# Another issue sequence for an attention and softplus-FFN kernel on one core

## The chip, the cores and the metric

The kernel runs on one core of a Trainium2 chip. The metric is the device time of one execution in microseconds (us), from several executions. A core has engines that each work through their own instruction stream in order: TensorE (PE, matmuls; its weight loads are listed as PEld), VectorE (DVE), ScalarE (ACT), GpSimd (POOL) and SyncE (SP), on whose queue this kernel issues all of its DMAs.

## The reference

Attention over 4 batches, 8 heads, 768 positions of 64, then a feed-forward network (FFN) on the 3072 tokens of 512 values, in fp32:

```python
k_sum = k.reshape(B, H, nb, block, D).max(axis=3)      # block = 32, nb = 24
v_sum = v.reshape(B, H, nb, block, D).mean(axis=3)
scores_l = scale * np.matmul(q, k.transpose(0, 1, 3, 2))
mask_l = np.abs(pos[:, None] - pos[None, :]) < window   # window = 16
scores_s = scale * np.einsum('bhsd,bhnd->bhsn', q, k_sum) + np.log(block)
scores_all = np.concatenate([np.where(mask_l, scores_l, -1e9), scores_s], axis=-1)
a = np.exp(scores_all - scores_all.max(axis=-1, keepdims=True))
a = a / (a.sum(axis=-1, keepdims=True) + 1e-9)
attn = np.matmul(a, np.concatenate([v, v_sum], axis=2))
x = attn.transpose(0, 2, 1, 3).reshape(B * S, H * D)
h = x @ w_in                                            # 512 x 2048
g = np.maximum(h, 0.0) + np.log1p(np.exp(-np.abs(h)))   # softplus
out = g @ w_out                                         # 2048 x 512
```

So each query sees its 31 neighbours and 24 summaries of blocks of 32 keys (maximum) and values (mean).

## The kernel before

**Numbers and precision.** An fp32 matrix product is made from three matmuls on values split into a high part (fp32r, a shortened fp32) and a low part (the rest): high by high, low by high, high by low. The weights arrive from the host as 64-bit words and are taken apart on the chip.

**Tasks.** The program does not issue instructions as it goes. An object `Order` collects 1603 tasks, each with a number, the buffers that it reads and writes and one or two ways to run it (each way on one engine). `Order.issue(SEQUENCE)` then issues them in the order of the words of a string. A word is the number of a task; the suffix `a` picks the second way, on another engine. Waits between engines follow from the buffers. Since each engine works through its tasks in the order of issue, the string alone fixes what stands behind what on each engine and on SP's queue.

**Work and names.** The 12 chunks (256 queries each) form the groups x = 0 (two chunks), 1 (one), 2 to 5 (two each) and 6 (one). `a2.0.0` is the attention of group 2, its chunk 0, head pairs 0 and 1; `f0.8` is FFN block f = 8 of 16 for group 0; `w8` are the weights of that block; `s1` are the summaries of batch 1. The FFN runs over (group, blocks): (0, 0 to 10), (1, 0 to 10), (0, 11 to 15), (1, 11 to 15), then groups 2 to 6 with all 16 blocks each.

- Attention of a chunk and two head pairs: load q, k and v windows (SP) and the summaries (`load_sums`); `k_sums` copies the key summaries beside the keys (L490, DVE or ACT); `scores` (L582, PE); `mask` (L595, DVE); `exp` (L603, ACT); `inverse` (L610, L611, DVE); `normalize` (L616, GpSimd, or DVE as the second way); then for the first group transposes on PE (L629, L633), otherwise `transpose` on DVE (L642), a DMA out to a buffer "squares" and four back; `values` (L673, PE); `high` (L689, ACT) and `low` (L693, DVE) write the split FFN input xh, xl.
- Weights of a block: two loads of 512 KB (w_in L722, w_out L719); `magnitude` (DVE L735, or ACT L738), `clamp` (L742), `shift` (L746) and `sign` (L750) on DVE; `tail` (ACT L756 or DVE); `add_tail` (GpSimd, L764); `high` (L768, ACT or DVE) and `low` (L775, DVE or GpSimd). For w0 and w1 the w_in half and the w_out half are converted apart.
- FFN of a block: `product` (L804, PE, 12 matmuls into a PSUM bank "ph", of which there are two, shared with `values`, the warm matmuls and the first sums of v); `rounded` (L824, ACT softplus, the high part), `exact` (L828, ACT) and `rest` (L832, DVE, the low part); `project` (L841, PE) first with the high part, then with the low part. At the end of a group's blocks `read` (L872, L876) takes the result from PSUM and L893 stores it.
- Summaries of a batch: four loads of keys (L339) with a maximum on DVE (L325), four loads of values (L347, "st") with `sum_v` (L353 to L358, GpSimd, or DVE as the second way), `mean` (L365). For batch 0 the sums of v are matmuls (L403) and the mean is on ACT (L416).
- 40 tasks of two matmuls on the identity (`warm`, L915) fill TensorE at the start.

The buffers of tag "t" (two in turn) hold in turn keys or values for the summaries, the weights in conversion and results on their way out, so a load into one of them waits until the user before is done.

Of the kernel before, what the change touches and what calls it, by code (L numbers as in the profile page):

```python
# [159 lines left out]
610a 430 420 251a 423 361 587a 431 259 295 252 590 421 253 613 362 254 360 614 256 363 432 365 411 434 424 412  # L160
615 433 257a 367 258 364 594 435 591a 373 368 616 598 617 299 366 369 374 370 371 375 595a 436 376 592 627 599a
372 437 606 628 377 629 380 438 381 378 439 382 593 383 271 631 379 440 441 445 285 442 272 451 273 446 275 274
443 447 596 452 600 444 630 448 276 453 612 449 454 618 260 457 300 619 277a 463 608 458 597 278a 459 450 464
460 455 636a 465 466 456 384 261 461 385 462 265 262 386 469 263 264 639 470 471 472 475 266 654 640 620 611 481
476 477 607 305 478 609 467 291 655 658a 653 468 482 267a 473 483 641 292 474 293 479 484 480 294 487 268 493
296 488 661 485 489 676 494 490 623 495 486 642 622 297 643a 491 621 675 281a 499 496 298a 677 644 492 508 680a
282 500 283 284 501 497 509 502 286 510 498 662 301a 516 511 287a 663 288 683 512 302 804 645 503 303 805 513
# [16 lines left out]
949 957 954 1089 1090a 1091 958 955 963 960 959 1092 964 1100 965 1101 1109a 961 1071 968 1072 1079 1081 1073
1093 1094 1095 1096 974 969 1080 1082 970 1084 971 1085 980 975 1103 1102 976 1104 977 1097 966 1105 1098 1107
1099 1106 1108 1112 981 1110 982 1111 967 1113 1232 972 1236 983 1114 973 978 979 984 1115 1116a 1117 985 986
1233 1118 1237 1234 1238 992 987 1119 1120 988 1121 989 990 993 1122 994 995 998 1235a 1239a 1242 1004 999 1000
1246 1001 1249 1250 1258 1251 1010 1005 1253 1006 1252 1243 991 996 1007 1247 1240 1016 1011 1012 1244 1248 1241
1261 997 1262 1002 1013 1263 1245 1003 1008 1009 1017 1014 1264 1265a 1266 1018 1015 1123 1019 1267 1275 1276
1284 1020 1124 1277 1021 1024 1125 1279 1278 1022 1025 1254 1023 1027 1026 1126 1028a 1268 1269 1270 1271 1029  # L190
1255 1134 1127 1257 1128 1256 1259 1129 1260 1287 1135 1136 1130 1288 1131 1132 1137 1289 1133 1138 1272 1139
1280 1281 1273 1290 1140 1283 1291a 1282 1285 1274 1286 1292 1146 1141 1293 1302 1306 1303 1142 1301 1143 1144
1147 1148 1149 1152 1294 1295 1296 1297 1158 1153 1154 1155 1298 1159 1160 1309 1304 1299 1305 1300 1145 1307
1310 1150 1308 1161 1311 1151 1156 1157 1162 1312 1313a 1163 1314 1164 1315 1324 1328 1325 1323 1170 1165 1316
1166 1317 1167 1168 1318 1171 1319 1172 1173 1176 1320 1177 1178 1331 1326 1321 1179 1327 1322 1169 1329 1332
# [797 lines left out]
```

## Time and profile before

| | |
|---|---|
| three runs | 640.96, 639.19, 639.84 us; median 639.84 |
| span of the profiled execution | 638.3 us, 11177 instructions |
| PE busy | 623.1 us (98%) |
| DVE, ACT, POOL busy | 277.6 (43%), 316.3 (50%), 75.6 us (12%) |
| mean granted TensorE clock | 0.991 |
| DMA | 86.51 MB, mean 136 GB/s |

The span runs from the first to the last instruction; the runs shown are 0.9 to 2.7 us above it, the median 1.5. In the profile's rows, "start us, us, engine line op out<-in" of a timeline is followed in brackets by the idle time before it and the engine (with its tile and line) that ended it. A row of the chain of work gives start, duration and what ran. A row of the groups ends with busy us, mean ns of one, and idle time before it. 40 digits of a slice row are tenths of busy time in 40 equal slices of the span.

### The profile page before, as it was taken

To read this page: it belongs to the slowest core of one execution; us is meant where nothing else is said; L and a number is where in the kernel's file an instruction comes from. 1 tells how busy PE (TensorE), PEld (TensorE's weight loads), DVE (VectorE), ACT (ScalarE), POOL (GpSimd) and SP (SyncE) were. 2 spreads that over 40 slices of the span, in tenths; PEclk is the share of its full clock that TensorE was granted. 3 is DMA by queue.
4 is the path that set the end of the run, shared out by engine and by line. 5 is a ranking of instruction groups with operands and counts; after the bars stand their busy time and mean duration, and the time that the engine had idled before them with its cause. 6 is when DMAs were issued, how large, how long until landed. Compare 5 with 4: busy or idle time off the path is not lost.

```text
span 638.3 us, 11177 instructions
## 1 busy us (share of the span) xinstructions
PE 623.1 (98%) x4284; PEld 505.5 (79%) x4284; DVE 277.6 (43%) x753; ACT 316.3 (50%) x762; POOL 75.6 (12%) x70
## 2 busy tenths in 40 slices
PE   7889999999999999999999999999999999999997
PEld 6576777888888888887777877787888888888996
DVE  5879988779643435213451445432411111341111
ACT  4879887479652555215472434462522222552222
POOL 3333322334201130001000030000000000000000
PEclk9889999999999999999999999999999999999999
DMA  9999699744668742141354653453300400311100
GB/s 291 247 262 324 234 224 248 218 139 117 210 201 243 222 139 88 63 134 42 137 167 116 179 143 106 130 145 107 98 1 0 139 1 0 109 57 60 48 1 34
DMA packets 86629, 86.51 MB, mean 136 GB/s; under 512 B 26704, under 2 KB 72368, under 8 KB 86576
## 3 DMA queue, kind: packets, MB, share of 16 engines
q1 hardware_dynamic: 86576, 85.80, 46.2%
q8 instruction: 34, 0.56, 0.3%
q14 instruction: 19, 0.16, 0.1%
HBM read 65.01 MB, written 18.35 MB: 131 GB/s over the span
## 4 chain that ended last, share of the span: by engine, by line
PE 91%; DMA 3%; ACT 3%; SPq 1%; DVE 1%; issue 0%; ACTq 0%
PE po L841 42%; PE ph L804 41%; PE xo L673 4%; PE sc L582 3%; DMA raw<-w_out_dram 2%; DMA k<-kT_dram 1%; ACT sp L603 1%; PE vt L403 1%; DVE sp L616 1%; ACT t L738 0%; SPq L722 0%; ACT pT L633 0%; PE pt L629 0%; ACT raw L756 0%; ACT w L768 0%
## 5 line engine op out<-in xcount | busy, mean ns | idle before, releaser
L804 PE MATMUL ph<-xh,w 128*128 128x512 f32 (+1 forms) x896 | 261.7, 365 | 4.0 <-DVE gl L832 2.5
L841 PE MATMUL po<-w,gh 128*128 128x512 f32 x768 | 204.8, 396 | 0.0
L804 PEld LDWEIGHTS ph<-xh,w 128*128 128x128 f32 x896 | 161.8, 189 | 35.0 <-DVE gl L832 3.1
L832 DVE TENSOR_TENSOR gl<-ph,gh 128x512 fp32r<-128x512 f32 (+1 forms) x112 | 68.2, 611 | 232.5 <-ACT ph L828 211.2
L841 PEld LDWEIGHTS po<-w,gh 128*128 128x128 f32 x768 | 142.3, 188 | 32.7 <-issue 0.8
L804 PE MATMUL ph<-xl,w 128*128 128x512 f32 (+1 forms) x448 | 163.0, 364 | 0.5 <-DVE xl L693 0.5
L824 ACT ACTIVATE gh<-ph 128x512 fp32r<-128x512 f32 (+1 forms) x112 | 60.2, 538 | 207.3 <-PE ph L804 169.3
L841 PE MATMUL po<-w,gl 128*128 128x512 f32 x384 | 115.6, 398 | 0.0
L804 PEld LDWEIGHTS ph<-xl,w 128*128 128x128 f32 x448 | 84.6, 189 | 16.2 <-DVE xl L693 1.3
L841 PEld LDWEIGHTS po<-w,gl 128*128 128x128 f32 x384 | 71.0, 188 | 17.1 <-issue 0.9
L603 ACT ACTIVATE sp<-sp,nm 128x120 f32<-128x120 f32 x192 | 73.1, 382 | 4.4 <-DVE nm L595 4.1
L828 ACT ACTIVATE ph<-ph 128x512 f32<-128x512 f32 (+1 forms) x112 | 59.4, 531 | 0.0
L764 POOL TENSOR_TENSOR t<-t,raw 128x1024 int32<-128x1024 int32 (+1 forms) x18 | 41.8, 2328 | 91.7 <-DVE t L750 26.3
L595 DVE CUSTOM_DVE_ANT_0 sp<-sc,added 128x120 f32<-128x120 f32 x192 | 40.7, 277 | 17.7 <-PE sc L582 17.3
L824 ACT ACT_TABLE_LOAD x24 | 30.8, 1283 | 34.0 <-PE ph L804 30.7
L693 DVE TENSOR_TENSOR xl<-xo,xh 128x512 fp32r<-128x512 f32 x24 | 16.5, 689 | 46.2 <-ACT xh L689 46.2
L603 ACT ACTIVATION_READ_ACCUMULATOR sp<-sp,nm 128x1 f32 x192 | 35.9, 187 | 0.0
L689 ACT CAST xh<-xo 128x512 fp32r<-128x512 f32 x24 | 14.1, 586 | 40.9 <-PE xo L673 40.9
L616 DVE TENSOR_TENSOR sp<-sp,ss 128x960 f32<-128x960 f32 x21 | 26.4, 1258 | 0.5
L673 PEld LDWEIGHTS xo<-pT,v 120*64 120x64 f32 x640 | 20.3, 138 | 7.5 <-issue 6.2
L642 DVE STREAM_TRANSPOSE tb<-sp 128x1024 f32<-128x1024 f32 x20 | 24.8, 1240 | 1.5 <-POOL sp L616 1.2
L353 POOL TENSOR_TENSOR st<-st 96x512 f32<-96x512 f32 (+1 forms) x10 | 10.1, 1011 | 127.9 <-DMA st<-v_hp_dram 127.5
(60 smaller groups left out, 379.4 us busy)
## 6 DMA issues: line engine op xcount, KB each, us to landing
squares<-tb SPq DMA_DIRECT2D x20, 512.0 KB
pT<-squares SPq DMA_DIRECT2D x80, 128.0 KB
raw<-w_in_dram SPq DMA_DIRECT2D x16, 512.0 KB
raw<-w_out_dram SPq DMA_DIRECT2D x16, 512.0 KB
kf<-kT_dram SPq DMA_DIRECT2D x16, 384.0 KB
out_dram<-ob SPq DMA_DIRECT2D x11, 512.0 KB
q<-qT_dram SPq DMA_DIRECT2D x20, 256.0 KB
st<-v_hp_dram SPq DMA_DIRECT2D x12, 384.0 KB
```

Of the source, the lines that this page charges most:

```text
L582: nc.tensor.matmul(unit(g * NU + h * NPAIR + i)[r * QW:(r + 1) * QW, k0:k1], lhsT=q[rows, w * QW:(w + 1) * QW], rhs=k[rows], start=True, s ...
L595: nc.vector.tensor_tensor_reduce(out=sp()[:, n], in0=unit(n), in1=added()[:, kinds.index((lows[w], lows[w + 1]))], scale=-SCALE, scalar=FL ...
L603: nc.scalar.activation(sp()[:, n], sp()[:, n], AF.Exp, bias=nm()[:, n:n + 1], scale=-1.0, accum_out=ss()[:, n:n + 1],)
L616: engine.tensor_tensor(sp(), sp(), s, op=ALU.mult)
L642: nc.vector.transpose(out=tb().rearrange("p k (u q) -> p u k q", q=SQ), in_=tiles.sp().rearrange("p u (k q) -> p u k q", q=SQ),)
L673: nc.tensor.matmul(xo()[h * D:(h + 1) * D, g * CH + w * QW:g * CH + (w + 1) * QW], lhsT=tiles.v(g)[:, w, h * D:(h + 1) * D], rhs=queries(g ...
L764: nc.gpsimd.tensor_tensor(a, a, word(0, I32), op=ALU.add)
L804: nc.tensor.matmul(ph()[:, :n_x], lhsT=w1()[:, i1, part, cc * P:(cc + 1) * P], rhs=a()[:, cc, :n_x], start=cc == 0 and i == 0, stop=cc == ...
L824: nc.scalar.activation(gh()[:, :n_x], ph()[:, :n_x], AF.Softplus)
L828: nc.scalar.activation(ph()[:, :n_x], ph()[:, :n_x], AF.Softplus)
L832: nc.vector.tensor_sub(out=gl()[:, :n_x], in0=ph()[:, :n_x], in1=gh()[:, :n_x].bitcast(F32),)
L841: nc.tensor.matmul(po[t](), lhsT=a()[:, t * P:(t + 1) * P], rhs=w2()[:, i2, part], start=f == f0 and i == 0, stop=f == f1 - 1 and i == 2,)
```

## The change

Only the string SEQUENCE differs: the same 1603 tasks and the same buffers are issued in another order, and 58 of them on another engine. Read engine by engine:

- **SP.** The first w_in halves of w0 (133) and w1 (151) are issued before the first q (64, 68), two loads of v (65, 97) come earlier among the loads of the first attention, and w4 (189, 190) precedes the other loads of v. Further on, more weight loads stand ahead of the k and v loads and squares of group 1.
- **PE.** 32 of the 40 warm tasks come ahead of the first scores (72). The set of tasks before the first FFN product (309) is the same. After it some neighbours change places: 314 before 325, 329 before 331, 330 before 337, 354 before values 410, scores 613 and project 360 before product 361, project 366 before product 373. In the later groups the scores of a chunk come several products earlier than before and pieces of attention stand side by side more often: 29 separate interruptions of the FFN's matmuls instead of 36.
- **DVE and ACT.** Rest 328 (f0.2) is issued ahead of mask 400 and normalize 403 (a1.0.0); before, it came behind them. Exp 106 (a0.0.2) now follows the tail of w0's w_out half (147). ACT and DVE exchange work: magnitudes 134, 143, 191, 231, 301, highs 167, 177, 297, k_sums 396, 422, 1083, 1109, 1486 and reads 382, 1024, 1025, 1226, 1445, 1448, 1449, 1599 go from ACT to DVE; highs 140, 149, 207, 287, read 800 and k_sums 907, 1035, 1258, 1284, 1328, 1460 from DVE to ACT. Transpose 404 is moved ahead of the conversion of w6.
- **GpSimd.** From DVE it takes normalizes 76, 665, 888, 914, 1064, 1090, 1116, 1265, 1291, 1335, lows 159, 168, 288, and the sums of v 587, 591, 595, 599 (batch 1) and 1235. DVE takes from it lows 141, 278, 298, 308, sums 866, 870, 1243 and normalize 1042. GpSimd has 44 tasks instead of 34, ACT 344 instead of 354, DVE 350 as before.

The head of the diff, up to the first FFN blocks:

```diff
 SEQUENCE = """
-0 2 64 3 43 4 45 5 68 6 133 7 160 8 51 1 9 47 132 10 44 11 49 12 13 46 14 55 15 72 96 53 16 134a 138a 17 73 151
-161a 74 162 100 84 135 163 142 164 136 137 57 18 165 85 139 19 59 20 166 52 48 86 61 75 76a 65 388 50 70 77 167
-21 396a 168 104 66 78 140a 156 141a 147 79 105 69 54 189 143a 56 152a 144 87 58 106 190 153 88a 60 62 145 154
-146 22 116 63 155 80 71 107 157 23 117 24 67 25 26 97 27 148 158 28 169 29 118 30 170 31 108a 32 101 33 34 98 35
-149a 99 36 159 37 38 103 39 150 40 102 119 191a 120a 81 179 195 192 89 91 193 90 180 41 92 194 82 93 128 171a 83
-196 130 42 94 109 131 111 95 110 199 112 172 309 391 175 173 129 174 197 200 113 389 176 392 121 114 387 123 122
-115 390 124 397 198 177 125 178 318 126 181a 219 127 220 185 182 239 310 183 240 201a 184 319 311 202 186 399
-312 320 414 313 269 205 325 209 203 187 204 413 321 188 225 416 314 415 326 206 322 315 417 327 400 316 210 221a
-317 270 323 207a 208 229 401 324 222 331 223 230 224 289 245 402 403a 329 241a 328 226 422a 332 404 337 405 242
-227 279 243 249 333 228 330 338 339 425 244 395 211a 335 334 246 340 215 343 212 235 406 213 247 214 336 344 248
-341 426 216 584 345 393 342 250 601 347 346 427 602 217a 604 407 218 348 585 588 349 394 398 231a 408 428 409
-290 232 355 350 603 233 234 351 589 236 353 356 352 357 586 605 358 410 429a 237 354 418 255 238 280 359 419
-610a 430 420 251a 423 361 587a 431 259 295 252 590 421 253 613 362 254 360 614 256 363 432 365 411 434 424 412
-615 433 257a 367 258 364 594 435 591a 373 368 616 598 617 299 366 369 374 370 371 375 595a 436 376 592 627 599a
...
+133 0 3 4 5 6 7 8 9 10 11 12 134 135 43 136 45 44 46 13 14 15 16 151 138a 2 17 1 137 152a 153 154 18 64 155 68 19 20
+139 21 22 140 156 23 24 25 26 27 28 29 141 30 31 32 33 34 157 72 35 36 37 160 51 165 47 38 39 100 53 49 73 161a 40 162
+163 164 52 84 65 74 96 41 54 55 166 48 57 158 59 97 85 42 50 104 167a 56 86 75 159a 58 142 61 76 105 147 143 106 144
+145 189 87 190 88a 77 60 69 79 116 62 78 63 132 146 168a 148 66 80 149 117 107 70 67 71 108a 191 150 118 192 119 81 89
+193 195 169 82 194 99 170 120a 90 91 92 196 101 98 93 171a 103 94 83 109 102 95 110 111 197 309 128 130 179 112 180
+113 172 388 173 175 174 114 121 123 122 124 125 198 199 115 176 396 185 126 177a 129 181a 200 392 127 318 178 131 387
+182 201a 183 310 311 390 312 184 319 202 389 313 320 391 321 322 397 239 393 219 205 399 314 398 220 186 203 325 204
+187 326 414 327 416 249 188 328 315 316 317 323 324 221a 206 400 240 394 222 422 225 395 209 210 223 329 413 331 207
+401 224 226 229 208 241a 332 417 242 330 227 243 402 403a 245 415 228 333 244 337 259 338 339 250 334 246 340 279 211a
+404 425 335 336 230 602 212 601 213 269 247 343 341 260 215 405 214 248 426 344 345 584 216 346 342 347 217a 270 406
+218 235 427 588 585 604 605 231 348 232 349 603 409 233 234 350 351 355 236 353 589 610a 352 265 356 407 237 408 428
+429a 357 238 586 280 354 410 411 358 587 430 251a 613 359 412 299 252 418 253 360 361 628 254 255 289 256 431 421 424
+614 367 590 362 432 257a 290 433 285 258 363 368 591 419 423 364 365 369 615 366 373 594 371 595 630 435 374 420 375
+434 598 370 372 436 437 376 599 616 629 300 377 592 438 617 378 381 382a 380 593 439 440 441 442 445 446 271 443 600
...
```

More of the change, by code (lines that the diff above doesn't have):

```diff
@@ L163 @@
[L163 to L167, printed above, removed]
@@ L184 @@
[L184 to L188, printed above, removed]
@@ L189 @@
[L189 to L193, printed above, removed]
@@ L194 @@
-1310 1150 1308 1161 1311 1151 1156 1157 1162 1312 1313a 1163 1314 1164 1315 1324 1328 1325 1323 1170 1165 1316
-1166 1317 1167 1168 1318 1171 1319 1172 1173 1176 1320 1177 1178 1331 1326 1321 1179 1327 1322 1169 1329 1332
-1174 1330 1333 1175 1180 1181 1182 1334 1335a 1336 1188 1183 1337 1184 1185 1186 1189 1190 1191 1194 1338 1339
[5 rows of a table removed]
-1463 1394 1477 1464 1478 1486a 1401 1480 1479 1465 1481 1399 1400 1402 1407 1466 1467a 1468 1403 1405 1404 1408
-1469 1409 1410 1406 1413 1470 1471 1472 1411 1414 1473 1415 1416 1412 1419 1474 1420 1421 1489 1482 1475 1422
@@ L204 @@
-1484 1476 1417 1483 1485 1490 1487 1418 1488 1491 1425 1423 1426 1492 1493a 1424 1431 1494 1427 1428 1495 1429
[6 rows of a table removed]
+133 0 3 4 5 6 7 8 9 10 11 12 134 135 43 136 45 44 46 13 14 15 16 151 138a 2 17 1 137 152a 153 154 18 64 155 68 19 20
+139 21 22 140 156 23 24 25 26 27 28 29 141 30 31 32 33 34 157 72 35 36 37 160 51 165 47 38 39 100 53 49 73 161a 40 162
+163 164 52 84 65 74 96 41 54 55 166 48 57 158 59 97 85 42 50 104 167a 56 86 75 159a 58 142 61 76 105 147 143 106 144
+145 189 87 190 88a 77 60 69 79 116 62 78 63 132 146 168a 148 66 80 149 117 107 70 67 71 108a 191 150 118 192 119 81 89
@@ new lines @@
+444 449 379 447 275 448 631 451 452 453 272 450 457 273 606 383 274 276 596 627 597 618 454 636a 458 639 459 295 277a
+460 455 278 384 619 261 262 263 385 456 463 464 469 653 609 465 470 654 471 264 655 461 466 386 266 607 462 475 467
+472 305 640 291 476 267a 477 641 478 612 292 293 468 473 474 479 480 481 268 487 658a 482 483 611 642 661 643a 294 676
+484 644 488 489 281a 490 485 675 282 493 296 297a 486 283 680a 620 645 494 499 284 491 495 500 496 492 501 502 497 286
+287 498 508 509 510 662 503 516 663 298 288a 517 518 301 511 512 504 302 623 621 303 622 677 683 804 807 304 505a 506a
@@ new lines @@
+507 803 513 514 522 664 519 306 307 812a 608 665 523 524 308 805 515 806 666 525 857 855 667 528 529 684 534 530 531
+624 815 520 685 858 646 648 647 686 856 687a 521 649 632 830 625 526 633 637 535 536 688 635 634 626 537 527 550 551
+552 638 650 829 532 553 816 533 538 689 651 838a 542 543 668 670 833 671 656 657 540 556 541 554 831 817 669 652 557
+558 539 832 659 818 544 562 563 660 859 559 672 841 545 555 673 678 564 674 565 819a 690 860 679 560 561 566 873 820
+875 568 692 691 682 567 693 681 569 570 574 571 876 575 572 874 694 576 573 695 577 546 578 842 872 580 821 696 808
@@ new lines @@
+881a 579 548 811 547 697 549 581 843 582 583 884 705 844 867 845 698 699 700 706 707 899 813 863 701 702 846 703 885
+708 901 898 822 868 886 704 902 825 864 1232 809 1233 814 824 711 907a 887 709 717 823 712 710 861 713 888 715 718 900
+847 810 719 714 862a 865 869 889 890 720 866a 870a 910 826 723 848 834 724 725 911 716 840 721 837 835 1031 827 1234
+836 839 912 1238 828 1032 726 722 729 730 851 1235 849 850 913 914 727 731 732 1239a 735 915 736 737 738 728 741 1242
+1035a 1030 852 1243a 1038 742 853 1246 877 733 743 1039 734 1040 739 744 880 891 1236 1041 740 1053 871 1054 1052 879
@@ new lines @@
+916 854 747 1057 892 1042a 748 1060 745 1247 746 1075 878 894 1237 749 1043 1078 1061 893 1074 882 750 751 752 1083
+883 1077 1076 1062 1244 1063 753 759 1044 754 755 760 761 1086 756 1064 1240 895 896 1065 757 1101 897 762 758 763 765
+1066 1087 917 764 1088 903 771 906 1248 1089 909 905 1104 766 908 767 904 920 918 1103 1102 768 919 772 1109 1241 1090
+921 1100 1112 1249 773 1250 922 923 769 1033 1037 1091 774 1258a 1113 770 1045 775 777 1036 1252 1092 776 783 778 779
+1046 1048 1251 781 1114 780 1115 784 789 1047 1253 782 1261 785 1116 786 790 791 1034 1276 1279 1049 1067 1245 792
@@ new lines @@
+1070 1275 787 788 796 1068 1055 795 1059 1284a 794 1050 1058 1117 1262 793 797a 1263 1056 1069 1277 924 800 801 925
+1051 1278 926 1118 932 1264 1287 927 1071 1079 1085 1093 798 1302 933 1265 934 1266 935 1288 928 929 1095 930 931 1289
+936 1084 1306 1096 1301 1072 937 1290 1073 1094 938 939 1081 944 1291 940 1267 1082 1292 945 1303 1080 946 1309 1323
+1324 941 1097 942 1098 1310 1105 943 1311 1106 1108 1325 948 1099 947 1312 1313a 1107 950 951 1328a 949 1111 956 1293
+1314 1331 952 953 1119 1122 1120 1121 799 957 958 1332 959 1110 1123 954 1124 955 962 1125 1333 960 1254 1255 1452
@@ new lines @@
+1460a 963 964 965 961 966 967 1315 968 969 974 1257 970 975 976 1334 1335 972 1260 1336 971 973 977 978 979 1268 980
+986 981 982 983 987 988 989 984 1451 1256 1259 802 985 990 992 1455 991 993 1269 994 1454 1270 995 998 996 999 1000
+1004 1005 1271 1001 1010 1006 1011 997 1007 1012 1013 1016 1337 1453 1463 1464 1272 1294 1297 1273 1280 1465 1274 1466
+1467a 1296 1286 1002 1003 1017 1018 1478 1008 1285 1009 1479 1281 1481 1019 1014 1015 1020 1022 1295 1283 1468 1486
+1282 1298 1299 1024a 1021 1304 1480 1023 1300 1307 1477 1126 1127 1128 1134 1129 1135 1316 1130 1317 1318 1136 1305
@@ new lines @@
+1140 1025a 1489 1137 1319 1308 1320 1490 1027 1469 1141 1142 1028a 1143 1131 1132 1326 1338 1330 1340 1133 1329 1341
+1491 1321 1327 1138 1339 1492 1139 1144 1322 1145 1342 1026 1470 1493a 1494 1343 1344 1146 1147 1152 1148 1149 1153
[3 rows of a table added]
+1210 1211 1212 1213 1218 1214 1215 1474 1219 1220 1221 1216 1217 1222 1345 1226a 1475 1223 1225 1482 1224 1346 1488
[5 rows of a table added]
+1445a 1503 1504 1448a 1449a 1505 1506 1509 1446 1510 1507 1511 1508 1512 1513 1514 1515 1516 1521 1517 1519 1522 1518
[3 rows of a table added]
+1593 1591 1589 1590 1592 1594 1595 1596 1598 1597 1599a 1600 1602 1601
```

11 lines of the change are left out of this document (removed), and 28 rows, old and new, of the table SEQUENCE.

## The prediction

> **What bounds the kernel now.** I read the head of the page first, for the span and the slices; then the busy time by window over the stages where the slices show gaps; then what TensorE waited for; then its timeline at each wait, beside the engine that ended it.
>
> ```profile
> span 638.3 us, 11177 instructions
> PE   7889999999999999999999999999999999999997
> 0.00:40.00 40.00, 32.34 (x437) 24.65 (x437) 27.70 (x103) 26.64 (x87) 13.53 (x32) 0.91 0.96 263
> 40.00:80.00 40.00, 36.71 (x260) 28.45 (x260) 35.13 (x58) 35.64 (x57) 14.70 (x7) 0.96 0.87 279
> 80.00:120.00 40.00, 39.44 (x263) 31.94 (x262) 32.16 (x75) 29.47 (x63) 8.52 (x4) 1.00 0.94 236
> 120.00:160.00 40.00, 40.00 (x308) 34.43 (x307) 31.69 (x76) 30.99 (x75) 18.13 (x7) 1.00 0.48 144
> ```
>
> Columns of a window: its length, busy time and count of PE, PEld, DVE, ACT, POOL, then granted clock, DMA share, GB/s. PE is busy 40.00 of 40 from 120 on, and the slices are 9 up to the last. PE idles 7.66 us (40 − 32.34) in the first window, 3.29 in the second, 0.56 in the third. An order of issue takes no matmul away, so it can win only there, where DMA shares are 0.96, 0.87 and 0.94 and VectorE and ScalarE are near 35 of 40, or in how densely matmuls follow each other. It can lose anywhere.
>
> ```profile
> PE ph L804 <- DVE gl L832: 2.5, 2, 1.3
> PE ph L804 <- ACT xh L689: 1.5, 1, 1.5
> PE xo L673 <- DVE gl L832: 0.6, 1, 0.6
> PE ph L804 <- DVE xl L693: 0.5, 2, 0.3
> 39.62 0.49 PE L804 MATMUL ph<-xh,w 128*128 128x512 f32 x1 [1.52 <-ACT xh L689]
> 53.97 0.50 PE L804 MATMUL ph<-xh,w 128*128 128x512 f32 x1 [1.20 <-DVE gl L832]
> 68.52 0.50 PE L804 MATMUL ph<-xh,w 128*128 128x512 f32 x1 [1.26 <-DVE gl L832]
> 92.89 1.15 PE L673 MATMUL xo<-pT,v 120*64 120x64 f32 x32 [0.56 <-DVE gl L832]
> ```
>
> The columns of the first four are total, times and longest wait. The feed-forward network (FFN) begins at 39.62 (task 309); after it PE loses 2.5 + 0.6 and part of 0.5. That is all that better placing of ScalarE and VectorE work can give back there.
>
> **The change, part by part.**
>
> *The start.* Warm matmuls (32 of 40) go ahead of the first scores; they cover idle PE and cost nothing by themselves. On SP, loads 133 and 151 pass the first q (64, 68), so 2304 KB instead of 1280 KB are asked for until q has landed: 1024 KB at 263 GB/s (first window), about 4 us later scores. Does that reach 39.62?
>
> ```profile
> 6.75 0.42 PE L582 MATMUL sc<-kf,first 64*64 64x96 f32 x8
> 31.18 6.69 DMA raw<-w_out_dram
> 37.97 1.14 ACT L738 ACTIVATE t<-raw 128x1024 f32<-128x1024 f32 x1 [1.41 <-DMA raw<-w_out_dram]
> ```
>
> The third row is magnitude 171 of weights w2, which waits for load 170; high 94, which starts the FFN, stands behind it on ScalarE in both orders. Ahead of 170 SP issues 9296 KB instead of 9344: 48 KB at 263 GB/s, 0.2 us earlier. So the weight load keeps the FFN where it is as long as the attention is no later. It has slack only because the loads of v (65, 97) pass others and ScalarE, now without magnitudes 134, 143, 191, does fewer conversions in between. I take 0. Bounds: −0.5 (0.2 and a shorter ScalarE queue) and +2.5 (the 4 us less the 1.5 that PE already waited). This cover gone, the late q is what comes next.
>
> *The waits after 39.62.* 53.97 (product 325 behind rest 313/322): the neighbours are reordered, project 314 comes ahead of 325; I take −0.1 (−1.2 to +0.3). The next, with VectorE and GpSimd beside it:
>
> ```profile
> 64.42 2.43 POOL L764 TENSOR_TENSOR t<-t,raw 128x1024 int32<-128x1024 int32 x1 [4.80 <-DVE ss L610]
> 64.55 3.32 DVE L616 TENSOR_TENSOR sp<-sp,ss 128x960 f32<-128x960 f32 x1
> 67.79 0.68 DVE L832 TENSOR_TENSOR gl<-ph,gh 128x512 fp32r<-128x512 f32 x1
> L616 DVE TENSOR_TENSOR sp<-sp,ss 128x960 f32<-128x960 f32 x21 | 26.4, 1258 | 0.5
> ```
>
> Normalize 403 takes 3.32 us where such a one takes 1.26 on average: it started 0.13 us after a GpSimd add_tail and lasted until shortly after that ended. Rest 328 stood behind it, and product 337 behind the rest. The change puts 328 ahead of mask 400 and normalize 403: −1.3 (bounds −1.26 and 0).
>
> What is late next? PE then reaches everything 1.3 us earlier, and the weights must keep up.
>
> ```profile
> 82.61 1.23 DVE L775 TENSOR_TENSOR w<-t,w 128x1024 fp32r<-128x1024 f32 x1
> 84.70 0.40 PE L804 MATMUL ph<-xh,w 128*128 128x512 f32 x1
> 90.30 2.03 PE L841 MATMUL po<-w,gh 128*128 128x512 f32 x8
> 90.58 0.68 DVE L832 TENSOR_TENSOR gl<-ph,gh 128x512 fp32r<-128x512 f32 x1
> ```
>
> Low 218 of w6 ends at 83.84, and product 349 that needs it starts at 84.70; 1.3 earlier it would be 83.4, so PE waits +0.4 (0 to +1.7: transpose 404, another 1.2, is moved ahead of w6 on VectorE). Rest 352 ends at 91.26. Project 354, now ahead of values 410, follows the projects of the third row: at 92.33, or 91.0 with the gain, which is 0.3 too early. Against this the 0.56 before 410 is covered by 354. Together −0.2 (−0.6 to +0.5).
>
> *Sums of v on GpSimd.* The four sums of batch 1 (587, 591, 595, 599) go there, among w10's and w12's conversion.
>
> ```profile
> L353 POOL TENSOR_TENSOR st<-st 96x512 f32<-96x512 f32 x5 | 6.4, 1286 | 127.5 <-DMA st<-v_hp_dram 127.5
> L353 DVE TENSOR_TENSOR st<-st 96x512 f32<-96x512 f32 x7 | 5.0, 716 | 3.7 <-DMA st<-v_hp_dram 2.8 <-DVE gl L832 0.8
> L353 POOL TENSOR_TENSOR st<-st 96x256 f32<-96x256 f32 x5 | 3.7, 735 | 0.4
> L353 DVE TENSOR_TENSOR st<-st 96x256 f32<-96x256 f32 x7 | 3.0, 422 | 0.2
> L355 POOL TENSOR_TENSOR st<-st 96x128 f32<-96x128 f32 x4 | 1.8, 458 | 0.3
> 103.45 0.69 DVE L768 CAST w<-t 128x1024 fp32r<-128x1024 f32 x1 [0.28 <-POOL t L764]
> 104.17 1.23 DVE L775 TENSOR_TENSOR w<-t,w 128x1024 fp32r<-128x1024 f32 x1
> 105.32 0.68 DVE L832 TENSOR_TENSOR gl<-ph,gh 128x512 fp32r<-128x512 f32 x1
> 109.20 1.09 PE L841 MATMUL po<-w,gl 128*128 128x512 f32 x4
> 103.77 5.60 PE ph L804 x24
> ```
>
> One sum costs GpSimd 1.29 + 0.74 + 2 × 0.46 = 2.9 us, and takes at least 0.72 + 0.42 = 1.1 off VectorE. The last five rows are high 257, low 258 and rest 364 on VectorE, then project 366, then two products (367, 373) that stood before 366. In the new order 373 follows 366: 366 comes up 2.8 us earlier (half of 5.60), at 106.4, and less the gains above (1.3 + 0.2 − 0.4) at about 105.3. Rest 364 ends at 106.0 in the old trace, and 257 now waits for an add_tail that is queued behind a sum which itself waits for a load of v. At no further delay 366 waits 0.7. At a full sum's 2.9 us of delay it waits 3.6. I take +2.0, near the middle, because VectorE is rid of 1.1 per sum ahead of 364 while its two-input instructions may be held up beside GpSimd as 403 was. Range of the term 0 to +5, the top with one more hold-up (up to 3.32 − 1.26 = 2.1) where the sums' buffers come free later and the keys of batch 1 load later.
>
> The Trainium skill, *SBUF — State Buffer*, "SBUF: two separate sides", says that VectorE with two SBUF inputs and a GpSimd operation share a pair of ports as an exclusive lock, and that whoever starts first holds it for the whole instruction. The rows at 64.42 and 64.55 agree: 3.32 us is about what is left of the 2.43, then a normalize. By that rule each of the ten tasks that the change adds on GpSimd can hold up a VectorE one, which speaks against the change.
>
> *Other conversions.* Clamps, highs and lows of w11 to w15 trade engines among rests 466 to 550; one late rest costs some 0.7 (the length of a rest): +0.5 (−0.3 to +1.5). The later normalizes on GpSimd (nine) and k_sums on ScalarE lie after 120, where PE never waits and where the scores of a pair now stand several products further ahead of its values than before: 0 (cover gone: one normalize of 1.26 at a time).
>
> *Density.* From group 3 on, attention pieces are put side by side between FFN matmuls: 29 separate interruptions instead of 36.
>
> ```profile
> 100.78 2.99 PE po L841 x12
> 109.36 2.80 PE po L841 x12
> ```
>
> Twelve matmuls of the same form take 2.99 behind a change of kind and 2.80 without: 0.2 each, 7 × 0.2 = −1.4 (−2 to 0: the price may come from the buffers and not from the change of kind).
>
> *The tail.* The last reads go one to ScalarE and one to VectorE.
>
> ```profile
> 633.99 1.28 ACT L876 COPY ob<-po 128x512 f32<-128x512 f32 x2 [1.37 <-PE po L841]
> ```
>
> The second read waits for the last project in both: 0 (−0.3 to +0.2).
>
> *Sum:* 0 − 0.1 − 1.3 + 0.4 − 0.2 + 2.0 + 0.5 − 1.4 + 0 = −0.1 us. The span would be 638.2. The median of the three runs shown, 639.84, is 1.5 over the profiled span; with that offset 639.7.
>
> **The rivals.**
>
> *Slower: GpSimd's sums decide.* Place: rest 364 before project 366, and what follows it (inverse 616, values 436, product 439). For it: the 3.32 us row, and a VectorE busy 32.16 of 40 there. Against: in the new order VectorE has 1.1 us less per sum. From +4 of delay on (one sum of 2.9 and half a hold-up of 2.1) instead of my 2.0 it decides: 638.2 + 2 to + 5 gives 640.2 to 643.2, at the median's offset 641.7 to 644.7; as one number 642.7. A start late by up to 2.5 ends in the same place, 642.2.
>
> *Faster: no new wait.* The gains stand (−1.3 − 0.5 − 1.4 − 0.1 = −3.3) and the losses stay below 0.5 each way, since VectorE is less loaded: 636.5. For it: VectorE is idle 8 to 9 us of 40 after 80, by the windows, so a hold-up need not reach a rest. Against: w6 has 0.86 us of slack only.
>
> *Nothing reaches the end.* The weight loads at DMA shares of 0.87 to 0.96 set both the start and the rests up to 120; each wait taken away turns up one stage later, and density brings nothing: 639.8.
>
> **How the numbers follow.** About 0.3% (1.9 us) is what a measurement of this kernel tells from no change: 637.9 to 641.8. My forecast 0.34 and "nothing" 0.13 lie within; "faster" 0.24; "slower" 0.29 (sums 0.19, start 0.10). Of the forecast's own range (638.2 to 641.2) nearly all is inside. So faster 0.25, same 0.45, slower 0.30. The range goes to the faster case's 636.5 and to 643.4 in the slower one, which leaves out some 2 in 10.
>
> **What would show it.** First product between 39.1 and 40.5 with ScalarE's high or magnitude 171 named; the wait near 68 gone, with 328 ahead of 403; a wait of some 0.4 before 349; a project behind rest 364 that waits 1 to 3 us near 105, sums of 2.9 us on GpSimd at that time, and long two-input VectorE rows beside them; no PE idle from 120 to the end; mean matmul rows unchanged but fewer 2.99 pieces. The prediction is wrong if PE starts the FFN later than 42, if 366 waits over 4 us, or if waits appear after 120, where I put none.

## The result, and the profile after

| | before | new order |
|---|---|---|
| runs beside each other | 639.19 us median (638.56 to 640.96, five runs) | 646.62 us median (644.78 to 647.78, five runs) |
| ratio | | 1.0106 (95% interval 1.0087 to 1.0124) |
| again, on another occasion | 640.74 us | 645.43 us, ratio 1.0077 (1.0057 to 1.0097) |
| profiled execution | span 638.3 us | span 643.0 us, 644.78 us in all |

The new order is slower by 0.8 to 1.1%, outside the predicted range of 636.5 to 643.4. The profiled execution was the fastest of its five. What follows explains the 4.7 us of its span (643.0 against 638.3); the controls further down show where the timed loss of 4.7 to 7.4 us lies. Lines of the source are 3 lower than before (product L801, project L838, scores L579, values L670). First the head of the page and two windows of TensorE's busy time, of the new order:

```profile
span 643.0 us, 11191 instructions
PE   8789999999989899999999999999999999999997
160.00:200.00 40.00, 38.11 (x354) 31.73 (x353) 21.39 (x68) 20.34 (x59) 3.66 (x4) 1.00 0.75 207
200.00:240.00 40.00, 38.25 (x239) 30.53 (x239) 22.53 (x76) 25.20 (x70) 7.82 (x6) 0.96 0.91 253
```

The same two windows of the kernel before:

```profile
160.00:200.00 40.00, 40.00 (x364) 33.30 (x363) 21.85 (x75) 21.33 (x58) 2.94 (x1) 1.00 0.68 217
200.00:240.00 40.00, 40.00 (x228) 32.28 (x227) 14.78 (x40) 20.28 (x53) 10.12 (x12) 1.00 0.66 189
```

TensorE (second number) was never idle there; now it idles 1.89 and 1.75 us. The DMA share of the second window rises from 0.66 to 0.91, and its granted clock (third number from the end) falls from 1.00 to 0.96. TensorE's timeline after the change, every row with an idle time from the first product on except three between 39 and 48 us that stand in the old trace too (0.2 to 0.3 us each) and two of 0.2 or less:

```profile
39.17 0.50 PE L801 MATMUL ph<-xh,w 128*128 128x512 f32 x1 [1.38 <-ACT xh L686]
50.59 1.56 PE L579 MATMUL sc<-k,q 64*64 64x120 f32 x32 [0.46 <-DMA q<-qT_dram]
52.64 0.74 PE L838 MATMUL po<-w,gh 128*128 128x512 f32 x2 [0.49 <-ACT gh L821]
53.86 0.50 PE L838 MATMUL po<-w,gl 128*128 128x512 f32 x1 [0.48 <-DVE gl L829]
111.14 1.15 PE L670 MATMUL xo<-pT,v 120*64 120x64 f32 x32 [1.01 <-DMA st<-v_hp_dram]
189.12 1.15 PE L670 MATMUL xo<-pT,v 120*64 120x64 f32 x32 [1.64 <-DMA kf<-kT_dram]
221.58 0.42 PE L579 MATMUL sc<-k,q 64*64 64x120 f32 x4
223.75 1.64 PE L579 MATMUL sc<-k,q 64*64 64x120 f32 x28 [1.75 <-DMA k<-kT_dram]
```

The waits at 68 and 93 us are gone and the one at 54 has become three of about 0.48 around 50 to 54. New are those at 111 (values 436), 189 (values 672) and 224 (scores 910, which had issued four of its 32 matmuls). All three wait for DMAs. The tiles that the rows at 111 and 189 name (`st`, `kf`) are not what these values read; by the landings in the trace, values 436 started 0.04 us after a `pT` load from the squares had landed (issued at 105.82), and values 672 0.02 us after the second of their two `load_sums` (659 and 660, issued at 184.39 and 185.25, landed at 188.77 and 189.10). In the old trace these two were issued at 181.66 and 183.08, and values 672 ran at 187.4 without a wait: here TensorE comes no earlier, the loads come later.

Scores 910 stood at 245.1 in the old trace; the new order has them at 221.6, 24 us earlier. The chain of work of the new order shows what their keys waited for:

```profile
212.41 5.19 DMA k<-kT_dram
217.62 6.08 DMA k<-kT_dram
223.75 1.64 PE sc L579 x28
```

The last load of keys (900) was issued at 217.62, 0.02 us after the landing of the load issued at 212.41 (902), which fills another part of the same buffer; it took 6.08 us itself. Between the two stand seven other DMAs, two of them 384 KB loads for the summaries of batches 2 and 3. One of these (1232, keys of batch 3) was issued at 213.5 where the old order has it at 353. Four of the eight summary loads of batch 3 (1.6 MB) lie between 200 and 240 us now, all eight behind 350 before; the window moves 2.6 MB more than before (253 against 189 GB/s).

Scores 910 and values 826 are also slow once they run: they take 3.81 and 1.98 us from their first start, where such pieces take 0.98 and 1.08, and only 1.75 of that is the wait. Short windows of the new order, and one of the order before, show why:

```profile
224.00:226.00 2.00, 2.00 (x40) 1.70 (x34) 1.92 (x4) 0.00 (x0) 0.00 (x0) 0.51 0.44 157
226.00:228.00 2.00, 2.00 (x29) 1.80 (x26) 1.93 (x5) 0.00 (x0) 0.00 (x0) 0.64 0.82 266
228.00:230.00 2.00, 2.00 (x11) 1.61 (x10) 1.86 (x6) 0.00 (x0) 0.00 (x0) 1.00 0.96 286
```

```profile
40.00:44.00 4.00, 3.77 (x32) 2.71 (x33) 2.81 (x4) 2.55 (x4) 1.07 (x2) 0.57 1.12 271
```

The granted clock is 0.5 for 3.4 us from 224.03 on, which costs half of that. The old trace has one such stretch too, from 40.33 on; this trace of the new order has none there. So half clock cancels in this pair of profiles. In others it does not: of the eleven profiles, this one and those of the runs below, whose orders hold the new words from 560 to 892, six have a stretch of 3.4 or 6.8 us at 0.5 between 224 and 236 us. The profiles of h1, cut560, cut740, start_only, mid_only, best1 and best2 have none between 49 us and the last matmul.

The ledger of the two profiled executions, by the starts of TensorE's matmuls. A start counts as late by what exceeds the usual distance: 0.232 us behind an FFN matmul of 512 columns, 0.120 behind one of 256, 0.98 and 1.08 for a whole piece of scores and of values.

| | before | new order | difference |
|---|---|---|---|
| first product | 39.62 | 39.17 | −0.45 |
| lateness at waits, to 105 us | 5.0 | 3.4 | −1.6 |
| lateness at waits, after 105 us | 0 | 5.7 | +5.7 |
| lost at half clock | 1.6 | 1.6 | 0 |
| all other late starts | 8.0 | 8.9 | +1.0 |
| behind the last matmul | | | +0.1 |

The sum is +4.7. The idle times in the brackets add up to less (3.84 to 2.17 before 105 us, 0 to 4.8 after), in part because idle time begins at the end of the matmul ahead, and that end is modelled.

### The profile page after: what moved, and what is told of

Same layout as the page of the kernel before. It is cut to its first block, busy times and chain, and to the rows that moved or that the text cites. A ratio compares the mean times of both kernels' runs of the same rounds, so it can differ in the third digit from the quotient of the medians.

```text
span 643.0 us, 11191 instructions
## 1 busy us (share of the span) xinstructions
PE 624.1 (97%) x4284; PEld 506.1 (79%) x4284; DVE 274.8 (43%) x749; ACT 308.7 (48%) x752; POOL 94.6 (15%) x84
## 4 chain that ended last, share of the span: by engine, by line
PE 83%; DMA 8%; SPq 3%; DVE 2%; ACT 2%; issue 1%; POOL 0%; ACTq 0%
PE po L838 38%; PE ph L801 37%; PE xo L670 3%; PE sc L579 3%; DMA raw<-w_in_dram 2%; DMA k<-kT_dram 2%; DMA pT<-squares 1%; DMA first<-v_hp_dram 1%; DMA st<-v_hp_dram 1%; SPq L497 1%; PE vt L400 1%; DVE sp L592 0%; SPq L651 0%; ACT t L735 0%; DMA kf<-kT_dram 0%
## 5 line engine op out<-in xcount | busy, mean ns | idle before, releaser
L801 PE MATMUL ph<-xh,w 128*128 128x512 f32 (+1 forms) x896 | 261.1, 363 | 1.4 <-ACT xh L686 1.4
L838 PE MATMUL po<-w,gh 128*128 128x512 f32 x768 | 206.4, 398 | 0.8 <-ACT gh L821 0.5
L801 PEld LDWEIGHTS ph<-xh,w 128*128 128x128 f32 x896 | 161.1, 188 | 32.1 <-ACT xh L686 1.9
L838 PEld LDWEIGHTS po<-w,gh 128*128 128x128 f32 x768 | 141.2, 188 | 35.5 <-ACT gh L821 1.9
L801 PE MATMUL ph<-xl,w 128*128 128x512 f32 (+1 forms) x448 | 162.4, 363 | 0.5 <-DVE xl L690 0.5
L838 PE MATMUL po<-w,gl 128*128 128x512 f32 x384 | 114.6, 395 | 0.5 <-DVE gl L829 0.5
L801 PEld LDWEIGHTS ph<-xl,w 128*128 128x128 f32 x448 | 84.3, 188 | 16.2 <-DVE xl L690 1.1
L838 PEld LDWEIGHTS po<-w,gl 128*128 128x128 f32 x384 | 71.7, 188 | 18.0 <-DVE gl L829 1.5
L761 POOL TENSOR_TENSOR t<-t,raw 128x1024 int32<-128x1024 int32 (+1 forms) x18 | 43.4, 2409 | 76.1 <-DVE t L747 21.9
L613 POOL TENSOR_TENSOR sp<-sp,ss 128x960 f32<-128x960 f32 x12 | 21.5, 1792 | 146.7 <-DVE ss L608 137.2
L670 PEld LDWEIGHTS xo<-pT,v 120*64 120x64 f32 x640 | 21.2, 142 | 8.5 <-issue 5.5
L670 PE MATMUL xo<-pT,v 120*64 120x64 f32 x640 | 24.1, 230 | 2.9 <-DMA kf<-kT_dram 1.6
```

What stands on the lines that cost most here:

```text
L613: engine.tensor_tensor(sp(), sp(), s, op=ALU.mult)
L670: nc.tensor.matmul(xo()[h * D:(h + 1) * D, g * CH + w * QW:g * CH + (w + 1) * QW], lhsT=tiles.v(g)[:, w, h * D:(h + 1) * D], rhs=queries(g ...
L761: nc.gpsimd.tensor_tensor(a, a, word(0, I32), op=ALU.add)
L801: nc.tensor.matmul(ph()[:, :n_x], lhsT=w1()[:, i1, part, cc * P:(cc + 1) * P], rhs=a()[:, cc, :n_x], start=cc == 0 and i == 0, stop=cc == ...
L838: nc.tensor.matmul(po[t](), lhsT=a()[:, t * P:(t + 1) * P], rhs=w2()[:, i2, part], start=f == f0 and i == 0, stop=f == f1 - 1 and i == 2,)
```

## The experiments

Each kernel is the old program with another string. Theory A: TensorE meets scores and values whose loads SP issues too late. Theory B: the work moved to GpSimd delays buffers, and through them SP. Ratios are to the kernel before on the same occasion.

**Where the loss arises.** The first words of one order, then the words left in the other.

```diff
-SEQUENCE = all words of the old order
+SEQUENCE = first 400 words of the new order (to about 105 us), rest in the old        # h1
+SEQUENCE = first 400 words of the old order, rest in the new                          # h2
+SEQUENCE = first 560 (740, 892, 1200) words of the new order, rest in the old         # cut560, cut740, cut892, cut1200
```

> The first 400 words of the new sequence (up to about 105 us), then the words left in the old order. Theory A (late data): the new order gains until about 105 us (first FFN product 0.45 us earlier, waits at 54, 68 and 93 us shortened, 2.8 us in all) and loses only later, where scores and values meet loads that SP issued too late. Then this is 639.2 - 2.8 = 636.4 us (635.5 to 638). Theory B (GpSimd): the sums of v of batch 1, of which three of four are on GpSimd in this first part, delay the buffers and so SP; then this is 640 to 643.

Measured: 639.56 us, 0.9998 (0.9985 to 1.0012), the range of neither theory. The trace shows no wait at project 366 beside the sums, which speaks against theory B before 105 us. This trace takes 2.9 us less than the old one from the first product to the last matmul, but that product starts 2.0 us later (41.57), and the timed gain of 2.8 us is missing.

> The first 400 words of the old sequence, then the words left in the new order. Theory A: all of the loss and none of the gain, 646.6 + 2.8 = 649.4 us (647 to 651). Theory B: of the GpSimd work only the later normalizes and one sum of batch 1 are left, so at most 1 to 4 us of loss: 640 to 643.

Measured: 653.51 us, 1.0205 (1.0181 to 1.0228). The loss lies behind word 400. It is 4.1 us above the 649.4 expected; the trace shows a wait of 4.06 us at 119, where the two orders join.

> The first 560 words of the new sequence (values 436 at 111 us are in them, values 672 and scores 910 are not), then the words left in the old order. Theory A: between the run of 400 words (no change) and the new kernel; with the 1.0 us wait before 436 added: 641.0 us (640 to 642). If the loss is spread evenly over the order instead: 642 to 643.

Measured: 640.39 us, 1.0002 (0.9990 to 1.0014). The wait before values 436 that the 641.0 counts is not in its trace.

> The first 740 words of the new sequence (values 672 at 189 us are in them, scores 910 with values 826 at 222 us are not), then the old order. Theory A: 1.7 us more than with 560 words, 642.8 us (641.5 to 644); what is left to the new kernel (646.6), some 3.5 us, is the place of 910 and 826. If the loss lies after 290 us, or is spread evenly: 644 or more is not reached, 642 or less, or 644 to 645.

Measured: 642.38 us, 1.0035 (1.0019 to 1.0051).

> The first 892 words of the new sequence (to about 270 us; scores 910 and values 826 are in them), then the old order. Theory A, that the loss is complete at 222 to 228 us: 1.010 times the kernel before, 646.4 us (645 to 647.5). If a part of it lies later, in waits that the one trace does not show: 643 to 645.

Measured: 643.82 us, 1.0056 (1.0036 to 1.0077). This is below theory A's range and in that of its rival.

> The first 1200 words of the new sequence (to about 400 us), then the old order. Theory A: as with 892 words, less some 0.3 us of denser matmuls: 646.2 us (645 to 647.5). If it comes out 1 us or more above the run of 892 words, the order loses beyond 270 us too.

Measured: 644.00 us, 1.0049 (1.0029 to 1.0070), no more than with 892 words, and again below theory A's range.

These left open whether the new order loses beyond 892 words as well (1.005 against 1.011). So the new order and its first 892 words ran on one chip:

> The new order itself, on one chip with the run of its first 892 words. In the traces the new order and its first 892 words take 599.7 and 598.8 us from the first product's start to the last matmul's, so theory A has the loss complete by 290 us and expects both within 1 us of each other, at 1.005 to 1.011 times the kernel before. If the new order past 290 us loses in executions that were not profiled, it is 2 us or more above the other.

> The first 892 words of the new sequence, then the old order, again, beside the new order on the same chip: 1.0056 (1.0036 to 1.0077) was measured. Theory A: within 1 us of the new order. Else 2 us or more below it.

Measured: 645.43 us, 1.0077 (1.0057 to 1.0097), for the whole; 648.20 us, 1.0107 (1.0077 to 1.0136), for the 892 words. The two came out 2.8 us apart and not within 1 us, the 892 words being the slower. So no loss is to be seen behind them: it begins after word 560 and is there by word 892, between about 160 and 270 us. The same kernel differs by 0.3 to 0.5% from one occasion to the next (1.0056 and 1.0107; 1.0106 and 1.0077), so that differences of that size between occasions prove nothing, and a loss or gain of 2 us behind word 892 stays possible.

A part of that spread is the granted clock. The two profiles of the 892 words have spans of 643.1 and 648.6 us; the first has no half clock between 105 us and the last matmul, the second 6.8 us of it from 228.9 on, and a longer stretch of it at the first product as well. Together these cost the second 4.5 us more. Its six executions run from 642.96 us at a mean granted clock of 0.996 to 650.43 at 0.984. The clock is not the whole loss: on this occasion the mean is 0.990 for the new order and 0.992 for the kernel before, some 1.3 us of 640, where the loss is 4.7.

The new order itself was profiled a second time here (span 645.2). Its waits after 105 us come to 7.8 us of lateness, 3.9 of it between 215 and 235: 2.25 us inside scores 910, as before, and then 1.27 before a product that needs a rest of VectorE's. The wait before values 436 is not there.

TensorE's windows 160 to 200 and 200 to 240 show the same place within single executions. First the run of 560 words, then that of 740:

```profile
160.00:200.00 40.00, 39.05 (x330) 31.91 (x330) 25.49 (x81) 22.95 (x61) 4.81 (x2) 1.00 0.65 203
200.00:240.00 40.00, 40.00 (x254) 32.18 (x254) 14.43 (x38) 18.77 (x51) 10.15 (x12) 1.00 0.66 190
```

```profile
160.00:200.00 40.00, 38.39 (x327) 31.91 (x326) 22.74 (x61) 22.04 (x59) 6.25 (x5) 1.00 0.74 208
200.00:240.00 40.00, 40.00 (x256) 32.08 (x255) 15.84 (x55) 18.68 (x52) 7.67 (x9) 1.00 0.61 187
```

The 0.95 us that the run of 560 words idles in its first window are at the joint (163 to 164 us). The waits at 188 and before values 672 come with the words up to 740; idle time in the second window comes only with those up to 892, and with it the DMA share of 0.9.

**GpSimd.**

```diff
-... 587 ... 591 ... 595 ... 599 ...
+... 587a ... 591a ... 595a ... 599a ...      # pool_dve: sums of v on VectorE
-... 665 ... 888 ... 914 ... 1335 ...
+... 665a ... 888a ... 914a ... 1335a ...     # norm_dve: nine normalizes on VectorE
```

> The new order with the four sums of v of batch 1 (587, 591, 595, 599) on VectorE instead of GpSimd, nothing else. Theory A: the trace shows project 366 without a wait beside these sums, so no change, 645.6 to 647.6 us. Theory B, and my term of +2.0 us in the prediction: 2 to 4 us faster, 642.6 to 644.6.

Measured: 647.39 us, 1.0126 (1.0100 to 1.0153): not faster. The timelines of TensorE and of VectorE in this run:

```profile
106.73 2.07 PE L838 MATMUL po<-w,gl 128*128 128x512 f32 x4 [3.55 <-DVE gl L829]
```

```profile
104.30 1.14 DVE L350 TENSOR_TENSOR st<-st 96x512 f32<-96x512 f32 x2
105.47 0.29 DVE L352 TENSOR_TENSOR st<-st 96x128 f32<-96x128 f32 x1
105.79 0.29 DVE L353 TENSOR_TENSOR vs<-vs,st 96x128 f32<-96x128 f32 x1
106.00 0.68 DVE L829 TENSOR_TENSOR gl<-ph,gh 128x512 fp32r<-128x512 f32 x1
```

Here project 366 does wait, 3.55 us. Of these, 1.7 are the sum that now stands on VectorE ahead of rest 364 (104.30 to 106.00); the conversion ahead of it is late by another 1.7 (its low part starts at 103.15, against 101.46 below).

> The new order with the nine later normalizes (665, 888, 914, 1064, 1090, 1116, 1265, 1291, 1335) on VectorE instead of GpSimd. Theory A: it is the order of loads and of TensorE's pieces, not these: no change, 646 to 647.5. Rival: a normalize takes 1.79 us on GpSimd and 1.16 on VectorE, so transposes, squares and the loads behind them on SP are late by as much; then 1 to 3 us faster, 643.6 to 645.6.

Measured: 645.75 us, 1.0080 (1.0062 to 1.0099), between the two results of the new order (1.0106, 1.0077). Its trace has the waits at 189.5 (1.63 us) and 224.1 (1.72) unchanged. The gain of 1 to 3 us that theory B expects of this part is not there, as far as differences between occasions allow.

**Data and their use.**

```diff
-436 437 438 ahead of 377 378;  672 ahead of 555 560;  910 826 ahead of 723
+377 378 ahead of 436 437 438;  555 560 ahead of 672;  723 ahead of 910 826      # pe_late
-831 832 833 ahead of 659 660;  900 898 901 902 apart, behind 863, 1232;  861 ahead of 900;  630 ahead of 434
+659 660 ahead of 831 832 833;  899 898 901 902 900 together;  861 behind 823;  630 behind 434   # sp_front
+both                                                                            # fix_both
```

> The new order with three attention pieces later on TensorE alone: values 436 behind projects 377 and 378, values 672 behind projects 555 and 560, scores 910 (and values 826) behind product 723. The other engines' orders are the new ones. Theory A: the waits of 1.0, 1.6 and 1.75 us in front of them are filled, 646.6 - 4.4 = 642.2 us (641 to 644). Theory B, or a chain in which each wait filled comes back at the next piece: 645.5 to 647.

Measured: 644.25 us, 1.0061 (1.0038 to 1.0084). Against the new order's 1.0106 and 1.0077 that is a gain of 1 to 3 us, of 4.4 expected. The trace shows none of the three waits at its old place, but 1.06 us before another values task at 199, 0.85 before product 723, 0.76 before values 826 and 0.68 at 233.

> The new order, with loads moved on SP's queue alone: the summaries of a2.1.0 (659, 660) ahead of the keys of a3.0.2 (831 to 833), the keys and q of a3.1.2 (898, 900 to 902) right behind 899, sums load 861 behind the squares of a3.0.0, keys 630 behind squares 434. Theory A with SP's order as cause: the waits of 1.6 us before values 672 and 1.75 us before scores 910 go, 646.6 - 3.4 = 643.2 us (642 to 645). Rival: TensorE reaches these pieces too early whatever SP does first, since SP's queue is full there; waits move to the neighbours, 646 to 647.5.

Measured: 645.38 us, 1.0070 (1.0050 to 1.0091). Against 1.0077 and 1.0106 that is a small gain or none. Windows of this run:

```profile
160.00:200.00 40.00, 39.90 (x363) 33.29 (x363) 23.24 (x73) 21.93 (x60) 5.16 (x5) 1.00 0.81 222
200.00:240.00 40.00, 37.01 (x233) 29.10 (x232) 22.29 (x72) 24.35 (x69) 7.69 (x6) 0.96 0.89 254
```

The wait before 672 is gone: 39.90 of 40, against 38.11. The load order was its cause. In the second window the keys of 910 are in time too, yet TensorE idles 3.0 us instead of 1.75. Its rows there, and those of VectorE:

```profile
220.67 2.13 PE L838 MATMUL po<-w,gh 128*128 128x512 f32 x8 [1.03 <-ACT gh L821]
224.99 0.69 PE L670 MATMUL xo<-pT,v 120*64 120x64 f32 x16 [0.60 <-DMA v<-v_hp_dram]
227.03 0.50 PE L801 MATMUL ph<-xh,w 128*128 128x512 f32 x1 [1.36 <-DVE gl L829]
```

```profile
222.79 1.81 DVE L350 TENSOR_TENSOR st<-st 96x512 f32<-96x512 f32 x2 [0.59 <-DMA st<-v_hp_dram]
225.17 1.23 DVE L639 STREAM_TRANSPOSE tb<-sp 128x1024 f32<-128x1024 f32 x1
226.33 0.65 DVE L829 TENSOR_TENSOR gl<-ph,gh 128x512 fp32r<-128x512 f32 x1
```

Values 826, right behind 910, wait 0.60 us for a load of v. The longest wait, 1.36, is for a rest that stands on VectorE behind a sum of v, which had itself waited for its load, and a transpose. With a DMA share of 0.89, what is moved forward is followed by waits at its neighbours.

> The new order with both earlier edits at once: scores 910, values 672 and 436 later on TensorE, and SP's loads for them forward. The two gave -2.4 and -1.2 us. If data and their use are both the cause, the waits left by each alone (0.8 before 723, 0.8 before 826, 1.4 before 723 again) go too: 642.0 us (641 to 643.5). Rival, that one wait is only passed on: as the better of the two, 644 to 645.

Measured: 643.96 us, 1.0060 (1.0044 to 1.0075). As good as the better of the two, the rival's case: the second window has 38.01 of 40, at a DMA share of 0.90. So the loss there is not one load or one piece alone. That the DMAs are asked for more in this stretch than before fits all these windows, but no run moved the summary loads of batch 3 back and left the rest, so that this is the cause is not shown.

**The first 105 us.**

```diff
+SEQUENCE = first 168 words of the new order, rest old                                  # start_only
+SEQUENCE = first 176 old words, then the new order to its word 400, rest old           # mid_only
+mid_only with 434, 435 ahead of 594 on SP                                              # best2
+best2 with 201, 202 behind 311, 312, 313 and values 436 behind project 372             # best1
+SEQUENCE = first 892 words of the old order, rest new                                  # late_only
```

> The first 168 words of the new sequence (loads of w_in and v moved up, warm matmuls first, up to the first FFN product), the words left in the old order. The prediction's term was 0: the same as before, 640.1 us (639.5 to 640.8). Rival, since the product began at 39.2 in the new kernel and at 41.6 in the run of its first 400 words: the new start is later on average and hides what the next 60 us gain; then 641 to 642. Second rival: it is earlier by the 0.45 us of the one trace, 639.6.

Measured: 640.53 us, 1.0000 (0.9985 to 1.0014): no change, as predicted.

> The old start (176 words), then the new order from the first FFN product to about 105 us, then the old order. If the waits at 54, 68 and 93 us are gone for good: 640.1 - 3.0 = 637.1 us (636.5 to 638.3; the run of the first 400 words took 3.0 us less from its first product to its end). Rival: each wait taken away comes back at the next piece, as in that run's median: 639.5 to 640.5.

Measured: 639.61 us, 0.9989 (0.9977 to 1.0001). The waits of 1.20, 1.26 and 0.56 us are gone from its trace, and there are 0.46 and 0.48 at 55, 0.26 at 106 and 1.18 at 113 us instead: −3.02 + 2.38 = −0.6, about as timed (−0.7). Most of a wait taken away came back within 60 us.

> The old start and the new order from the first product to 105 us, with only the squares 434, 435 ahead of loads 594, 630 on SP (for the 1.18 us before values 436). If that wait goes: 639.5 - 1.1 = 638.4 us, ratio 0.997. If SP's order was not its cause: as without the edit, 0.999.

Measured: 639.81 us, 0.9986 (0.9972 to 0.9999). The wait of 1.18 before values 436 is gone and 1.15 us stand before product 439, behind it, instead. At 0.14% this is the best order here, within what can be told from no change.

> The run with the old start and the new order from the first product to 105 us, with three edits for the waits that its trace shows: magnitude 201 and clamp 202 of w5 behind softplus 311, 312 and rest 313 (for 0.46 + 0.48 us at 55), values 436 behind project 372, and squares 434, 435 ahead of loads 594, 630 on SP (for 1.18 at 113). If the waits go: 639.5 - 2.0 = 637.6 us, ratio 0.996. If they are passed on: 639 to 640.

Measured: 640.77 us, 1.0004 (0.9990 to 1.0018): a miss. The two further edits brought waits of 1.38 us at 74 (behind w5, whose conversion they delayed) and 1.85 before the same product 439, since values 436 now came later.

> The old order for 892 words (to about 290 us), then the new one. Denser matmuls (attention pieces side by side) without the waits at 111, 189 and 224 us: the prediction's -1.4 us, of which the traces show -0.9 over the whole: 639.2 to 639.8. Rival: data of the attention come late there too, 641 or more.

Measured: 676.69 us, 1.0561 (1.0541 to 1.0582). This says nothing about dense matmuls: at the joint TensorE's next pieces are scores that the new order has far ahead, and their data were not there (waits of 12.43, 5.45 and 4.77 us for q and of 6.80 for maxima of keys, between 288 and 314 us). It shows how far ahead of its data such a piece can be put.

## Why the prediction was wrong

**The step that failed** is "0" for everything after 120 us, where "PE never waits" and scores stand "several products further ahead". I priced the normalizes and copies that changed engine there. I did not price when SP's queue brings the data of the pieces, which I had followed only up to 40 us. Two things had changed. Scores 910 came 24 us earlier, and their last keys were issued at 217.62 and took 6.08 us. Values 672 came no earlier, but the loads of their summaries were issued 2.7 and 2.2 us later. In place of 0 the profiled execution shows 4.5 us of lateness at waits after 120 us (1.2 more stand before values 436 at 111), and 1.6 us of half clock behind one of them. In the timed executions the loss of 0.8 to 1.1% arises between words 560 and 892. The two named causes are shown, since moving the loads or the pieces ends these waits; but it won back only 0 to 3 us, and why the neighbours then wait is open, as said at fix_both.

**Sums of v on GpSimd, +2.0:** too large, and so was its rival. In 11 of the 14 profiles with the new order up to there project 366 waits 0.2 to 1.2 us; in the first profile of the new order it does not. That profile's timelines of VectorE, GpSimd and TensorE at that place:

```profile
101.46 1.23 DVE L772 TENSOR_TENSOR w<-t,w 128x1024 fp32r<-128x1024 f32 x1
102.60 1.28 DVE L829 TENSOR_TENSOR gl<-ph,gh 128x512 fp32r<-128x512 f32 x2
```

```profile
102.53 2.12 POOL L350 TENSOR_TENSOR st<-st 96x512 f32<-96x512 f32 x2 [1.84 <-DMA st<-v_hp_dram]
```

```profile
103.43 1.10 PE L838 MATMUL po<-w,gl 128*128 128x512 f32 x4
```

Rest 364, the first of the two in the second row, ends at about 103.3, and project 366 starts at 103.4 without a wait. Two rests take 1.28 us beside a running sum on GpSimd, 0.64 each, no longer than elsewhere (0.68). The Trainium skill, *SBUF — State Buffer*, "SBUF: two separate sides", limits its lock to VectorE operations in a two-port mode or with two inputs in SBUF; a rest has one of its inputs in PSUM, so the page and this row agree, and I had applied the rule too widely. I also left out the other side of the exchange: on GpSimd this sum waited 1.84 us for its load without holding a rest, and on VectorE a sum stood 1.7 us ahead of the rest (pool_dve).

**The start, 0:** right (1.0000). But my bounds took one trace for a fixed time. The first product begins at 39.6 to 42.1 us in the profiles with the old start and at 38.8 to 42.6 in those with the new one. From there on TensorE ran 3.4 us at half clock in all profiles with the old start, and 0 to 6.5 us in those with the new one. No term had this, though the 0.96 of the window from 40 to 80 us showed it.

**The waits to 105 us:** 68 and 93 us right (gone); 54 became three parts of 1.43 in all, +0.2 where I had −0.1, within its range. The +0.4 before product 349 did not come: low 218 ended at 82.8, 1.0 us earlier than before, and the product began at 82.6, since only its third matmul reads the low part; my premise that its start waits for 218 was wrong. In sum I had −1.2 us for these waits; the one profile shows −1.6 to −1.7 up to 105 us, and the timed run of this stretch alone −0.7 (0.9989): mid_only's trace gives most of it back by 113 us.

**Other conversions, +0.5:** no such wait in the trace. **Density, −1.4:** direction right, size −0.6: the pauses of some 0.1 us that follow an FFN matmul where a foreign piece begins or ends sum up to 6.9 us before and 6.3 now. They cost 0.1 each, not 0.2.

**The tail, 0:** from the last matmul's start to the end of the span 4.05 us before and 4.1 after.

**The rivals.** The slower one had the right sign and the wrong place; that its 642.7 is nearer to the measured time than the forecast is luck. The case that held in the first 105 us was "nothing reaches the end": what is won at one wait is lost at the next.

## What to carry to other kernels

When an order moves work earlier on the engine that bounds the kernel, price the data's arrival there first: when the queue that loads them reaches those loads, and how full the DMAs are in that stretch; an engine that never waits has everything to lose. Here a wait that was taken away from a stretch in which the DMAs were busy 80 to 100% was mostly handed on to the next piece; take the gain from a run of the edit alone, not from the length of the wait. Look at the granted clock behind each wait too: 1.75 us of waiting was followed by 3.4 us at half clock, which cost as much again. Join two orders to find where a loss arises, and keep an eye on the joint, which can cost more than the effect.

## What the runs showed of the hardware

SP's queue never had more than eight DMAs under way. Its 401 DMAs tell of their landing by eight semaphores in turn, and in the traces of both orders no issue comes before the DMA eight places ahead has landed. In the new order 34 issues come within 0.06 us of that landing, in the old one 14. One is load 900, above. SP stood 2.2 us, until 183.47, behind the landing of a 512 KB load issued at 176.68, and its next two issues were released in the same way, the second of them `load_sums` 659, in these rows of the chain:

```profile
178.25 6.12 DMA pT<-squares
184.37 0.02 issue
184.39 0.81 SPq L497
```

So the limit met here is that of the program's eight semaphores; whether the chip has one as well is not shown.

TensorE's granted clock was 1.00 or 0.5, and each stretch of 0.5 between two of 1.00 lasted a multiple of 3.41 us: most 3.41 or 6.83, one 13.65 (mid_only) and one 37.55 (late_only). It fell behind a wait of 1.75 us in the first profile of the new order, and did not behind 1.64 us there, nor behind 2.25 us in the second profile. What decides it is not shown.

Beside a GpSimd operation a tiny VectorE one was slow: adding a constant to 128 x 8 values took 1.03 us where the median is 0.17, and ended with an add_tail that ran from 87.36 to 89.83.

```profile
88.83 1.03 DVE L607 TENSOR_SCALAR ss<-ss 128x8 f32<-128x8 f32 x1
```
